# V's place as a fourth weight buffer for every other FFN group, in a fused adaLN, attention and SwiGLU kernel

## The chip, the cores and the metric

The kernel runs on one core of one Trainium2 chip. The metric is the device time in microseconds (us) of one execution, as a median of several runs. "TensorE" is PE in the profile, "VectorE" is DVE, "ScalarE" is ACT, and SPq is the queue on which the SyncE sequencer issues DMAs.

## The reference

Cut to what matters (S = 2048 rows, D = 1024, F = 3584, bf16):

```python
h = _layernorm(x) * (1 + ca) + sa
x = x + ga * attention(h, k_cache, v_cache, wq, wo)   # 32 heads, last 512 keys
h = _layernorm(x) * (1 + cb) + sb
x = x + gb * ((silu(h @ w_gate) * (h @ w_up)) @ w_down)
```

## The kernel before

The rows are done in four chunks of 512 (`cc` = 0 to 3). Attention for all chunks comes first; then the FFN, chunk by chunk. For each chunk the FFN runs over 7 groups (`fg`) of 512 columns of F. A group needs four weight tiles of 512 KB: two of `w_gate` (wg) and two of `w_up` (wu). They come from a pool of seven buffers:

```python
    pb_ = ctx.enter_context(tc.tile_pool(name="blkB", bufs=7))
    ...
    v_sb = const.tile([P, Hkv, WT, Dh + 32], BF16, name="v_sb")   # V, read by attention alone
    ...
    def load_gu(cc, fg):
        for nm, v in (("wg", wg_v), ("wu", wu_v)):
            for i in range(2):
                t = blkB(nm, [P, 4, 512])
                load(t, v[:, 4 * i:4 * i + 4, fg * 512:(fg + 1) * 512])
                gu_w[(cc, fg, nm, i)] = t

    def emit_gu(cc, f):                      # f = 4 * fg + fi, 28 of them a chunk
        ...
        ps = big("gu_ps")                    # two buffers in PSUM
        for n, nm in enumerate(("wg", "wu")):
            for dt in range(DT):             # 8 matmuls each
                nc.tensor.matmul(ps[:, n, :], lhsT=gu_w[(cc, fg, nm, dt // 4)][...],
                                 rhs=hT[("h2", cc)][:, dt, :], ...)
        nc.scalar.activation(out=g, in_=ps[:, 0, :], func=ACT.Silu)
        nc.vector.tensor_tensor(out=guT[(cc, fg)][:, fi, :], in0=ps[:, 1, :], in1=g, op=ALU.mult)
```

While the first FFN chunk runs, the second layer norm of the last chunk (`cc` = 3) is still being made. VectorE writes the normalized rows xn; four DMA transposes on SPq turn them into hT.

## Time and profile before

| what | before |
|---|---|
| time, median of the first 3 runs | 1285.66 us (1285.42 to 1287.39) |
| span of the profiled execution | 1282.7 us |
| PE busy | 99% |
| first gu_ps matmul / last d_ps matmul starts at | 673.97 / 1277.20 us |

The page's first part gives the engines' busy time and share of the span; its fourth part says what the last chain of waits consists of:

```profile
PE 1269.7 (99%) x7601; PEld 642.9 (50%) x7601; DVE 577.8 (45%) x1271; ACT 333.9 (26%) x433; POOL 1.2 (0%) x8
...
PE 95%; DMA 2%; DVE 1%; SPq 1%; ACT 0%; issue 0%; DVEq 0%
```

Matmuls overlap (each counts 0.379 us, at 0.216 us from start to start), so a busy share hides gaps. Starts are better to read. This is the timeline of PE (start, length, engine, line, operation, count, and in brackets the idle time before it and what ended it):

```profile
749.94 1.89 PE L1168 MATMUL gu_ps<-hT,wg 128*128 128x512 bf16 x8
751.66 1.03 PE L1168 MATMUL gu_ps<-hT,wu 128*128 128x512 bf16 x4
754.79 1.04 PE L1168 MATMUL gu_ps<-hT,wu 128*128 128x512 bf16 x4 [2.10 <-DMA wu<-in_B_w_up_dram]
755.66 1.89 PE L1168 MATMUL gu_ps<-hT,wg 128*128 128x512 bf16 x8
```

Eight matmuls take 1.72 us, 0.216 us each from start to start. The fourth wu matmul of f = 16 starts at 752.31, the fifth not at 752.53 but at 754.79. (The profile counts idle time from the modelled end of a matmul, 0.379 us after its start. So its 2.10 us of idle is a start-to-start distance of 2.48 us, and 2.26 us are lost.) The list of PE's waits after 640 us has this wait alone:

```profile
PE gu_ps L1168 <- DMA wu<-in_B_w_up_dram: 2.1, 1, 2.1
```

The timeline of SPq shows why the load came late:

```profile
732.00 0.37 SPq L664 DMA_DIRECT2D wu<-in_B_w_up_dram  x1
...
743.56 6.84 SPq L848 DMA_TRANSPOSE hT<-xn  x4
750.50 0.53 SPq L664 DMA_DIRECT2D wu<-in_B_w_up_dram  x1
```

The wu at 732.00 is the fourth tile of group 3, issued alone as soon as a buffer came free. That of group 4 could have gone at about 747.5, but it stands behind four transposes and goes at 750.50. Issuing these four takes the queue 6.84 us.

### The profile page before, as it was taken

What the parts mean: (1) busy time and instruction counts of PE and PEld (TensorE: products, weight loads), DVE (VectorE), ACT (ScalarE), POOL (GpSimd) and SP (SyncE); (2) the same over time, 40 slices, a digit from 0 to 9 for tenths busy, and PEclk for the clock granted to TensorE, in tenths of its full rate; (3) what the DMA queues carried; (4) which work ended last, traced back from release to release, by engine and by line L of the source; (5) the groups of instructions that cost most, each with busy time, mean ns of one, the idle gap of its engine ahead of it and who ended that gap; (6) DMA issues with size and microseconds to landing.
All of it is one profiled execution on the core that took longest, in us unless ns stands there. A gap on an engine that the chain in (4) does not pass through costs nothing.

```text
span 1282.7 us, 18139 instructions
## 1 busy us (share of the span) xinstructions
PE 1269.7 (99%) x7601; PEld 642.9 (50%) x7601; DVE 577.8 (45%) x1271; ACT 333.9 (26%) x433; POOL 1.2 (0%) x8
## 2 busy tenths in 40 slices
PE   8999999999999999999999999999999999999998
PEld 4555555555555555555554444444444444444444
DVE  4464467865577755576653642221212221221122
ACT  3543334333333433333341111011100111011100
POOL 0000000000000000000000000000000000000000
PEclk9999999999999999999999999999999999999999
DMA  9888476557355654445487484454536455454401
GB/s 293 269 204 232 152 154 167 141 149 195 91 129 155 144 148 140 123 142 131 132 207 221 142 234 150 140 189 147 181 102 216 143 165 164 135 193 134 146 21 48
DMA packets 280108, 204.21 MB, mean 159 GB/s; under 512 B 113865, under 2 KB 273609, under 8 KB 280018
## 3 DMA queue, kind: packets, MB, share of 16 engines
q1 hardware_dynamic: 275106, 198.78, 54.2%
q10 hardware_dynamic: 4912, 4.20, 1.0%
q8 instruction: 61, 1.00, 0.3%
q14 instruction: 29, 0.24, 0.1%
HBM read 174.08 MB, written 4.21 MB: 139 GB/s over the span
## 4 chain that ended last, share of the span: by engine, by line
PE 95%; DMA 2%; DVE 1%; SPq 1%; ACT 0%; issue 0%; DVEq 0%
PE gu_ps L1168 29%; PE a_ps L1096 17%; PE q_ps L1019 17%; PE d_ps L1188 15%; PE o_ps L1064 9%; PE s_ps L1032 8%; DMA wm<-in_w_mod_dram 1%; SPq L664 1%; DMA hT<-xn 0%; DMA modT<-row_d 0%; DMA wu<-in_B_w_up_dram 0%; PE row_ps L779 0%; PE q_ps L940 0%; DVE st L816 0%; SPq L848 0%; ACT pT L1034 0%
## 5 line engine op out<-in xcount | busy, mean ns | idle before, releaser
L1034 ACT ACTIVATE pT<-s_ps 128x1024 bf16<-128x1024 f32 x256 | 248.7, 1020 | 341.8 <-PE s_ps L1032 341.8
L1096 PE MATMUL a_ps<-wo,oT 128*128 128x512 bf16 x1024 | 241.9, 379 | 0.7 <-DVE acc L1102 0.7
L1019 PE MATMUL q_ps<-hT,wq 128*128 128x512 bf16 x1000 | 236.7, 379 | 0.3 <-DVE modT L755 0.3
L1168 PE MATMUL gu_ps<-hT,wu 128*128 128x512 bf16 x896 | 211.8, 379 | 2.1 <-DMA wu<-in_B_w_up_dram 2.1
L1168 PE MATMUL gu_ps<-hT,wg 128*128 128x512 bf16 x896 | 211.7, 379 | 0.0
L1174 DVE TENSOR_TENSOR guT<-gu_ps,sg 128x512 bf16<-128x512 f32 x112 | 77.4, 691 | 283.5 <-ACT sg L1173 283.5
L1173 ACT ACTIVATE sg<-gu_ps 128x512 bf16<-128x512 f32 x112 | 66.9, 597 | 490.9 <-PE gu_ps L1168 439.7
L1188 PE MATMUL d_ps<-wd,guT 128*128 128x512 bf16 (+2 forms) x952 | 194.2, 366 | 0.0
L916 DVE CAST qT<-q_ps 128x512 bf16<-128x512 f32 x128 | 88.3, 691 | 176.6 <-PE q_ps L1019 176.0
L1096 PEld LDWEIGHTS <-oT 128*128 128x128 bf16 x1024 | 99.9, 98 | 122.1 <-issue 1.9
L1019 PEld LDWEIGHTS <-wq 128*128 128x128 bf16 x1000 | 97.8, 98 | 117.8 <-issue 0.3
L1188 PEld LDWEIGHTS <-guT 128*128 128x128 bf16 x952 | 90.9, 98 | 102.9
L1064 PEld LDWEIGHTS <-pT 128*128 128x128 bf16 x2048 | 126.6, 98 | 30.6 <-issue 0.4
L1168 PEld LDWEIGHTS <-wu 128*128 128x128 bf16 x896 | 87.6, 98 | 108.1 <-DMA wu<-in_B_w_up_dram 2.6
L1168 PEld LDWEIGHTS <-wg 128*128 128x128 bf16 x896 | 87.7, 98 | 105.4
L1064 PE MATMUL o_ps<-v_sb,pT 128*128 128x130 bf16 x2048 | 137.1, 220 | 0.0
L1032 PE MATMUL s_ps<-qT,kT 128*128 128x512 bf16 x512 | 131.5, 379 | 0.6 <-ACT pT L1034 0.6
L1051 DVE TENSOR_TENSOR oq<-o_ps,rl 128x256 bf16<-128x256 f32 (+2 forms) x256 | 101.3, 420 | 4.3
L1192 DVE TENSOR_TENSOR f<-d_ps,gb_bc 128x512 f32<-128x512 f32 (+2 forms) x34 | 22.5, 661 | 147.0 <-PE d_ps L1188 147.0
L1104 DVE TENSOR_TENSOR acc<-a_ps,acc 128x512 f32<-128x512 f32 x64 | 44.1, 689 | 38.9 <-PE a_ps L1096 38.9
L1032 PEld LDWEIGHTS <-kT 128*128 128x128 bf16 x512 | 44.9, 98 | 31.7 <-issue 1.3
L816 DVE BATCH_NORM_STATS2 st<-x 128x6 f32<-128x512 bf16 x64 | 41.3, 680 | 2.9 <-DMA x<-in_A_x_dram 2.6
(75 smaller groups left out, 309.3 us busy)
## 6 DMA issues: line engine op xcount, KB each, us to landing
wq<-in_A_wq_dram SPq DMA_DIRECT2D x64, 512.0 KB, 4.1
wo<-in_A_wo_dram SPq DMA_DIRECT2D x64, 512.0 KB, 5.5
wg<-in_B_w_gate_dram SPq DMA_DIRECT2D x56, 512.0 KB, 5.1
wu<-in_B_w_up_dram SPq DMA_DIRECT2D x56, 512.0 KB, 3.8
wd<-in_B_w_down_dram SPq DMA_DIRECT2D x56, 512.0 KB, 6.4
wmr<-in_w_mod_dram SPq DMA_DIRECT2D x8, 1024.0 KB, 11.4
x<-in_A_x_dram SPq DMA_DIRECT2D x16, 256.0 KB, 5.7
wm<-in_w_mod_dram SPq DMA_DIRECT2D x4, 1024.0 KB, 10.5
```

What stands on the lines that cost most here:

```text
L916: nc.vector.tensor_copy(out=t, in_=q_ps)
L1019: nc.tensor.matmul(q_ps, lhsT=wq_tiles[(cc, h // 4, dt // 4)][:, dt % 4, (h % 4) * P:(h % 4 + 1) * P], rhs=hT[("h1", cc)][:, dt, :], start ...
L1032: nc.tensor.matmul(s_ps[:, i, :], lhsT=kT[:, kv, j * P:(j + 1) * P], rhs=qT[g], start=True, stop=True)
L1034: nc.scalar.activation(out=p[:, 2 * jj:2 * jj + 2, :], in_=s_ps, func=ACT.Exp, scale=scale)
L1051: nc.vector.tensor_tensor(out=dst, in0=ps[:, s0:s0 + cnt, 0:Dh], in1=sc, op=ALU.mult)
L1064: nc.tensor.matmul(o_slot["ps"][:, s_, :], lhsT=pT[g][:, j, t * P:(t + 1) * P], rhs=v_sb[:, kv, j, 0:VN], start=(j == 0), stop=(j == WT - 1))
L1096: nc.tensor.matmul(a_ps, lhsT=oT[(cc, 2 * q + i)][:, hh % 4, t * P:(t + 1) * P], rhs=wo_tiles[(cc, q, dh, i)][:, hh % 4, :], start=(hh == ...
L1104: nc.vector.tensor_tensor(out=acc[(cc, t)][:, dsl], in0=a_ps, in1=acc[(cc, t)][:, dsl], op=ALU.add)
L1168: nc.tensor.matmul(ps[:, n, :], lhsT=gu_w[(cc, fg, nm, dt // 4)][:, dt % 4, fi * P:(fi + 1) * P], rhs=hT[("h2", cc)][:, dt, :], start=(dt ...
L1173: nc.scalar.activation(out=g, in_=ps[:, 0, :], func=ACT.Silu)
L1174: nc.vector.tensor_tensor(out=guT[(cc, fg)][:, fi, :], in0=ps[:, 1, :], in1=g, op=ALU.mult)
L1188: nc.tensor.matmul(d_ps, lhsT=guT[(cc, f // 4)][:, f % 4, t * P:(t + 1) * P], rhs=wd_tiles[(cc, dh, f // 4)][:, f % 4, c0:c0 + w], start=( ...
```

## The change

V is not read after attention, so its place in the on-chip memory is free in the FFN. The intent is to give gate and up weights two full sets of four tiles: seven pool buffers, and V's place for the fourth tile of each odd group.

```diff
+    v_flat = v_sb.rearrange("p a b c -> p (a b c)")
+    v_blk = v_flat[:, 0:2048].rearrange("p (a b) -> p a b", a=4)
+
     def load_gu(cc, fg):
+
         for nm, v in (("wg", wg_v), ("wu", wu_v)):
             for i in range(2):
-                t = blkB(nm, [P, 4, 512])
+                spare = (cc * NFG + fg) % 2 == 1 and nm == "wu" and i == 1
+                t = v_blk if spare else blkB(nm, [P, 4, 512])
                 load(t, v[:, 4 * i:4 * i + 4, fg * 512:(fg + 1) * 512])
```

## The prediction

> **What bounds the kernel now.** TensorE. The page gives PE busy 1269.7 of 1282.7 us (99%), and the chain that ended last is 95% PE. Busy alone proves little; in the timeline eight 128x512 matmuls take 1.725 us, 215.6 ns each, at a granted clock of 1.00. [...] So in the FFN (from 674 us on) there is nothing to win but gaps between matmuls, and there is exactly one: at 752.3 us the next start comes 2.48 us later instead of 0.22 us. The list of PE's waits has it as the only one after 640 us: 2.1 us, "gu_ps <- DMA wu". PE's other idle time lies in the first 30 us, untouched.
>
> **Why that gap.** Seven buffers hold four tiles a group, so the fourth tile of a group can't be loaded until the first tile of the group before is read for the last time. The queue's timeline shows it: one wu alone is issued about 5.0 us before its need, lands in 3.8 us, and so arrives 1.15 us early, in group after group. Group 4 is the exception: its fourth buffer came free at 747.4 us, but in the queue's order it stands behind four transposes hT<-xn that are issued from 743.6 to 750.4 us as VectorE supplies xn. It was issued at 750.50, landed at 754.75 and was needed at 752.5.
>
> **What the change does.** No work is added: the same 112 gate and up loads of 512 KB, the same matmuls. In the built programs PE's order is the same; only the DMA queue's moves. All four tiles of a group now come in a row, two groups ahead, when the tiles of two groups before come free. By the order in the queue, group 4's four tiles are issued before the hT transposes (estimate: about 731 to 734 us, when group 2 ends, 18 us before use), group 5's just after them, at about 750.5, some 15 us before use.
> Risks: the first load into V's place waits for the last o_ps matmul (674.1 us) and stands ahead of four transposes oT<-oq, which were issued at 674.7 anyway and are needed about 20 us later. DMA share is 0.40 to 0.68 in these stages (windows).
>
> **How much is on the critical path.** Only the 2.1 to 2.3 us gap: it stands in the chain as DMA hT<-xn, then DMA wu, and from 754.79 us to the end the chain is PE without a pause. The other fourth tiles gain slack that nobody waits for.
>
> **Time.** 1285.66 - 2.3 = 1283.4 us, 0.2% faster. Range 1282.4 to 1285.2 (runs of before spread over 2 us). Faster by over 2%: 0.005; within 2%: 0.99; slower: 0.005.
>
> **What would show it.** PE's waits after 640 us: none (right), or the same or another DMA wait (wrong). Timeline at 750 us: gu_ps starts unbroken. wu loads issued over 10 us before use in every group. Clock and DMA bytes (204 MB) unchanged.
>
> **What would make it wrong.** A new wait elsewhere, from the moved order: oT transposes or wd loads late behind loads that wait for buffers, or hT transposes slowed by loads in flight, each seen as a PE wait for a DMA. Or matmuls that are slower when their weights lie where V was: mean start-to-start above 216 ns.

1285.66 us less the gap of 2.3 us is 1283.4 us. That nothing but gaps was to be won, because a matmul of this size could not start sooner after the last than these 215.6 ns, was the author's estimate.

## More of the kernel before

```python
    def ln_mod(key, dt, sc, sh):             # VectorE, needs the DMA transpose
        ln_affine(key, dt, hT[key][:, dt, :], sc, sh, False)

    def plan_late_ln(k, key, sc, sh):
        for t in range(QT):
            ...
            at(k + 10 + 2 * t, ln_rows, tt)          # xn
            at(k + 11 + 2 * t, ln_xpose, key, tt)    # DMA transpose hT<-xn on SPq
        at(k + 8, late_rstd)
        for dt in range(DT):
            at(k + 24 + dt, ln_mod, key, dt, sc, sh)
```

In the FFN the framework's scheduler is free to move these operations; it puts them much earlier than their step, beside f = 13 to 16 of the first chunk.

## The result, and the profile after

| | before | after |
|---|---|---|
| median, 6 runs each | 1286.62 us (1285.42 to 1288.03) | 1284.75 us (1283.85 to 1285.22) |
| ratio | | 0.9984, 95% interval 0.9971 to 0.9997 |
| span of the profiled execution | 1282.7 us | 1283.0 us |
| first s_ps matmul starts at | 26.46 us | 27.69 us |
| first gu_ps to last d_ps (starts) | 603.24 us | 601.96 us |

A ratio here is the mean time of one kernel's runs over that of the other's of the same rounds, so it is not quite the ratio of the medians.

The time lies in the predicted range. The two profiled executions differ the other way (1282.7 and 1283.0 us), because the first 30 us alone took 1.23 us longer in the second one, under a lower granted clock (0.94 before, 0.89 after, from the windows view), and a wait at about 91 us (see e11) another 0.26 us. So the FFN is compared by itself, from the first gu_ps to the last d_ps: 1.28 us shorter, where 2.26 us had been forecast.

PE's waits after 640 us, and PE's timeline, in the changed kernel:

```profile
PE gu_ps L1173 <- DVE guT L1179: 0.8, 1, 0.8
```

```profile
751.42 1.89 PE L1173 MATMUL gu_ps<-hT,wg 128*128 128x512 bf16 x8
753.15 1.89 PE L1173 MATMUL gu_ps<-hT,wu 128*128 128x512 bf16 x8
755.87 1.89 PE L1173 MATMUL gu_ps<-hT,wg 128*128 128x512 bf16 x8 [0.83 <-DVE guT L1179]
```

The load wait is gone: eight wu matmuls in a row at f = 16. But one step later, before f = 17, the start-to-start distance is 1.21 us, so 1.00 us are lost to a wait for VectorE. SPq did what was forecast. Group 4's two wu tiles go at 735.21, ahead of the transposes:

```profile
733.49 1.23 SPq L664 DMA_DIRECT2D wg<-in_B_w_gate_dram  x2
735.21 1.23 SPq L664 DMA_DIRECT2D wu<-in_B_w_up_dram  x2
736.94 3.96 SPq L664 DMA_DIRECT2D wd<-in_B_w_down_dram  x4
745.04 6.80 SPq L848 DMA_TRANSPOSE hT<-xn  x4
```

VectorE's timeline shows the new wait. First the kernel before, then the changed one:

```profile
749.06 0.69 DVE L1174 TENSOR_TENSOR guT<-gu_ps,sg 128x512 bf16<-128x512 f32 x1
752.46 1.38 DVE L856 TENSOR_SCALAR hT<-hT,modT 128x512 bf16<-128x512 bf16 x4 [2.71 <-DMA hT<-xn]
753.75 0.69 DVE L1174 TENSOR_TENSOR guT<-gu_ps,sg 128x512 bf16<-128x512 f32 x1
```

```profile
750.50 0.68 DVE L1179 TENSOR_TENSOR guT<-gu_ps,sg 128x512 bf16<-128x512 f32 x1
753.84 1.38 DVE L856 TENSOR_SCALAR hT<-hT,modT 128x512 bf16<-128x512 bf16 x4 [2.66 <-DMA hT<-xn]
755.14 0.68 DVE L1179 TENSOR_TENSOR guT<-gu_ps,sg 128x512 bf16<-128x512 f32 x1
```

Both kernels do the same: VectorE reaches the scale and shift of hT, waits there about 2.7 us for the DMA transposes, does four of them, and only then empties gu_ps of f = 15. The matmuls of f = 17 need that PSUM buffer, as there are two. In the kernel before, PE was waiting for the wu load at that very time, until 754.79, and guT was done at 754.44 (753.75 + 0.69), before PE came to f = 17. Without the load wait PE would have come there at 753.39 (751.66 plus 8 x 0.216): 1.05 us too early. So a second wait seemed to lie underneath the first. ScalarE had finished sg for this step at 750.74 in the kernel before and at 752.22 in the changed one (timeline of ACT), so it was VectorE, standing at hT until 752.46 and 753.84, that kept guT back.

### The profile page after: what moved, and what is told of

Read it like the earlier page. It is cut to its first block, busy times and chain, and to the rows that moved or that the text cites. A ratio compares the mean times of both kernels' runs of the same rounds, so it can differ in the third digit from the quotient of the medians.

```text
span 1283.0 us, 18137 instructions
## 1 busy us (share of the span) xinstructions
PE 1270.0 (99%) x7601; PEld 643.1 (50%) x7601; DVE 577.3 (45%) x1271; ACT 333.9 (26%) x433; POOL 1.2 (0%) x8
## 2 busy tenths in 40 slices
DMA packets 280108, 204.21 MB, mean 159 GB/s; under 512 B 113865, under 2 KB 273609, under 8 KB 280018
## 4 chain that ended last, share of the span: by engine, by line
PE 96%; DMA 2%; DVE 1%; SPq 0%; ACT 0%; issue 0%; DVEq 0%
PE gu_ps L1173 29%; PE a_ps L1096 17%; PE q_ps L1019 17%; PE d_ps L1193 15%; PE o_ps L1064 9%; PE s_ps L1032 8%; DMA wm<-in_w_mod_dram 1%; DMA hT<-xn 1%; PE q_ps L940 0%; DMA modT<-row_d 0%; PE row_ps L779 0%; SPq L664 0%; PE mod_ps L753 0%; DVE st L816 0%; ACT pT L1034 0%; PE h_ps L927 0%
## 5 line engine op out<-in xcount | busy, mean ns | idle before, releaser
L1173 PE MATMUL gu_ps<-hT,wu 128*128 128x512 bf16 x672 | 163.3, 379 | 0.0
L1173 PEld LDWEIGHTS <-wu 128*128 128x128 bf16 x672 | 65.8, 98 | 79.3
L1173 PE MATMUL gu_ps<-hT,v_sb 128*128 128x512 bf16 x224 | 57.5, 379 | 0.0
```

## The experiments

Theory A: the change removes the load wait of group 4, and only that load mattered; a wait of 1.0 us for VectorE, which had lain under it, comes to light. Its rivals: the new wait is made by the moved loads; the load was late for another reason; the eighth buffer helps everywhere a little. "FFN" in the table is the start of the first gu_ps to that of the last d_ps. "Lost" is the start-to-start distance less 0.216 us. Every run gave the correct result.

| run | time, median | before beside it | ratio (95%) | FFN | lost in the FFN, to |
|---|---|---|---|---|---|
| before (first trace) | | | | 603.24 | 2.26, DMA wu |
| after (first trace) | | | | 601.96 | 1.00, DVE guT |
| e1_before_mod | 1285.71 | 1287.35 | 0.9987 (0.9974 to 1.0001) | 604.79 | 2.13, DMA wu |
| e2_after_again | 1284.41 | 1287.35 | 0.9975 (0.9962 to 0.9989) | 601.71 | 0.75, DVE guT |
| e3_after_mod | 1283.24 | 1287.35 | 0.9966 (0.9953 to 0.9980) | 600.96 | 0 |
| e4_spare_g1_g3 | 1284.20 | 1287.35 | 0.9973 (0.9960 to 0.9987) | 601.71 | 0.75, DVE guT |
| e5_before_again | 1286.12 | 1285.52 | 1.0006 (0.9992 to 1.0019) | 603.00 | 2.03, DMA wu |
| e6_before_fill | 1285.70 | 1285.52 | 1.0001 (0.9987 to 1.0015) | 603.12 | filled |
| e7_before_b6 | 1302.18 | 1285.52 | 1.0156 (1.0114 to 1.0199) | 619.57 | 20 waits, DMA wu |
| e8_after_b6 | 1287.07 | 1285.52 | 1.0009 (0.9993 to 1.0024) | 605.23 | 2.58, DMA wu |
| e9_spare_g1 (one run) | 1286.36 | 1286.06 | | 604.98 | 2.31, DMA wu |
| e10_before_late | 1283.22 | 1286.06 | 0.9977 (0.9962 to 0.9993) | 600.96 | 0 |
| e11_after_mod_cb1 | 1282.22 | 1286.06 | 0.9970 (0.9956 to 0.9983) | 601.04 | 0.08, at f = 16 |

e1 to e4 ran on one chip, e5 to e8 on another, e9 to e11 on a third. e9 was profiled once and not timed further; its state is unknown.

### e1 and e3: the VectorE operations later, in the kernel before and in the changed one

The eight hT operations of the last chunk and the guT operations are held to the order in which the program names them. That puts the former into the FFN of the second chunk.

```diff
     def ln_mod(key, dt, sc, sh):
+        if key == ("h2", NTC - 1):
+            tc.keep_in_program_order(nc.vector.tensor_scalar(out=hT[key][:, dt, :], ...same...))
+            return
         ln_affine(key, dt, hT[key][:, dt, :], sc, sh, False)
 ...
-        nc.vector.tensor_tensor(out=guT[(cc, fg)][:, fi, :], in0=ps[:, 1, :], in1=g, op=ALU.mult)
+        tc.keep_in_program_order(nc.vector.tensor_tensor(...same...))
```

Expected of e1:

> Seven buffers as before, but the eight VectorE operations that finish hT (scale and shift after the DMA transposes) stand later in VectorE's order, so that no guT stands behind them at about 754 us. Theory A (a second wait, of VectorE behind the transposes, lay hidden under the load wait): the load wait stays, start-to-start gap 2.48 us at the second half of wu of group 4, nothing else; first gu_ps to last d_ps stays 603.2 us; time as before within 0.1%. Rival B (the second wait was made by the moved loads and has nothing to do with this order): the same here. Rival C (the late wu load was late because VectorE stalled, not because of the buffer and the queue): the gap shrinks below 1 us.

Measured: the load wait stayed, 2.13 us lost, with nothing else behind it. So VectorE's stall at hT had not made it, and rival C falls. (The edit leaves the xn operations in place, but once the first transpose had gone, the queue of the kernel before waited for them for 0.33 us alone.) The FFN was not 603.2 but 604.79 us. That surprise is in the next part.

Expected of e3:

> The changed kernel with the eight VectorE operations later, as in e1. Theory A: no gap over 0.235 us after 640 us, first gu_ps to last d_ps 600.7 us, that is the whole 2.48 - 0.22 = 2.26 us of before plus nothing; 1.0 us faster than the changed kernel. Rival B (the moved loads slow the transposes or PE in some other way): a wait of about 1 us is left at this place, under another name.

Measured: no wait of PE after 640 us is left, and the FFN takes 600.96 us. That is 603.24 less 2.26; the 600.7 in the expectation was a slip of the sum. VectorE's timeline in e3 shows guT waiting for nothing but ScalarE where it had stood behind hT:

```profile
750.02 0.69 DVE L1184 TENSOR_TENSOR guT<-gu_ps,sg 128x512 bf16<-128x512 f32 x1
751.65 0.69 DVE L1184 TENSOR_TENSOR guT<-gu_ps,sg 128x512 bf16<-128x512 f32 x1 [0.95 <-ACT sg L1183]
755.11 0.69 DVE L1184 TENSOR_TENSOR guT<-gu_ps,sg 128x512 bf16<-128x512 f32 x1 [2.76 <-ACT sg L1183]
```

The four kernels make a square: either cure alone leaves a wait (2.13 us with the VectorE order alone, 0.75 to 1.00 us with the buffer alone), both leave none. The moved loads are not to blame, as they are the same in e3.

### e2 and e4: the change once more, and V's place in two groups alone

> The changed kernel once more, beside the others on one chip. Both theories: one gap of 1.2 us (start to start) before the first matmul of f = 17, put down to DVE guT; first gu_ps to last d_ps 602.0 us, 1.26 us under before; time 0.1 to 0.2% under before, with the rest of the difference from the first 30 us.

Measured: one gap again, 0.97 us from start to start, so 0.75 us lost instead of 1.00; the FFN is 601.71 us. The size of this wait depends on when the transposes land: counted from the first gu_ps, the last one landed at 78.27 us in the first trace and at 78.01 us here, 0.26 us earlier, and the wait is 0.25 us shorter. The time came out 0.25% under before, more than the FFN explains; see below.

```diff
-                spare = (cc * NFG + fg) % 2 == 1 and nm == "wu" and i == 1
+                spare = cc * NFG + fg in (1, 3) and nm == "wu" and i == 1
```

> V's place is used by groups 1 and 3 alone, the other 12 odd groups have the seven buffers as before. Theory A (only group 4's load counted): as the changed kernel, one gap of 1.2 us at f = 17, first gu_ps to last d_ps 602.0 us, although the fourth tiles of groups 6 and later land with 1.15 us to spare again. Rival D (the eighth buffer helps a little in every group, for instance by relieving the DMA queue): longer than 602.2 us.

Measured: the same gap and the same FFN as e2, to 0.01 us, and a median 0.2 us apart. Twelve of the fourteen uses of V's place gain nothing that can be seen here.

### e9: V's place in group 1 alone

The same edit with `in (1,)`. SPq's order from group 2 on is then as before, and group 4's last tile stands behind the transposes again.

> V's place is used by group 1 alone; from group 2 on the DMA queue's order is as in before, so group 4's fourth tile is again issued behind the four hT transposes. Theory A: the load wait is back, start-to-start gap 2.2 to 2.5 us at wu of f = 16, first gu_ps to last d_ps 603.0 to 603.3 us (or 1.7 us more where the clock drops). Rival G (it is enough that the first groups are loaded earlier): a gap of 1.0 to 1.2 us put down to DVE guT, 601.7 to 602.0 us, as in e4.

The queue in e9's timeline, as it was in the kernel before:

```profile
743.69 6.90 SPq L848 DMA_TRANSPOSE hT<-xn  x4
750.69 0.53 SPq L664 DMA_DIRECT2D wu<-in_B_w_up_dram  x1
```

Measured in one look: the load wait is back, with 2.31 us lost, and the matmuls after it were slow again, as in e1 (eight took 2.90 us instead of 1.89; FFN 604.98 us). So it is the place of group 4's load in the queue that counts.

### e10: another order of the transposes, with no eighth buffer

The kernel before with e1's edit, and the four late xn operations held to program order too, which moves the transposes on SPq behind group 4's load. (The diff is cut to its new part.)

```diff
-            at(k + 10 + 2 * t, ln_rows, tt)
+            at(k + 10 + 2 * t, ln_rows, tt, True)   # True: xn kept in program order
```

> Seven buffers, no use of V's place, but the four xn operations and with them the hT transposes of the last chunk, and the hT scale and shift, keep their program order and so come later, after group 4's fourth tile. Theory A (the order in the DMA queue, not the number of buffers, made the wait): the 2.48 us gap at f = 16 is gone without the eighth buffer. The transposes now stand among other fourth tiles with 1.15 us to spare, so a smaller wait at another group is possible; I expect at most 1 us in all, first gu_ps to last d_ps 601.0 to 602.0 us. Rival H (seven buffers make group 4 late by themselves): the 2.48 us gap stays.

The queue in e10's timeline (cut):

```profile
747.50 0.37 SPq L664 DMA_DIRECT2D wu<-in_B_w_up_dram  x1
...
776.07 1.25 SPq L856 DMA_TRANSPOSE hT<-xn  x1
```

Measured: group 4's load went at 747.50, no wait after 640 us, FFN 600.96 us as in e3, and 1283.22 us (e3, on another chip: 1283.24). I had feared a smaller wait at another group; none came. Seven buffers are enough when the four transposes do not stand in a row ahead of a load that has about 1.15 us to spare. The eighth buffer makes the kernel indifferent to that order, which is another way to the same gain, but it cannot cure the VectorE wait.

### e7 and e8: one buffer fewer

```diff
-    pb_ = ctx.enter_context(tc.tile_pool(name="blkB", bufs=7))
+    pb_ = ctx.enter_context(tc.tile_pool(name="blkB", bufs=6))
```

> The kernel before with 6 buffers in place of 7, so two tiles a group, not one, come just in time. Theory A (7 buffers were enough everywhere else because the fourth tile lands 1.15 us early): now wu0 has about 4.1 us from issue to need and wu1 5.0 us, and a pair issued together lands in about 4.5 and 5.2 us, so PE waits about 1 us in each of some 21 groups without attention work beside them: first gu_ps to last d_ps about 620 to 625 us, time about 1.5% over before. Rival D (buffers hardly matter to this kernel): within 0.3% of before.

> The changed kernel with 6 buffers in place of 7: with V's place it has 7 in odd groups, so one tile a group comes just in time, as in before. Theory A: about as before with 7 (load wait of 2 us at group 4, first gu_ps to last d_ps 603 to 605 us), so here the same change is worth about 1.5% against e7. Rival D: equal to e7.

PE's waits after 640 us, e7 first, then e8 (what waited for what, us in total, times, longest):

```profile
PE gu_ps L1168 <- DMA wu<-in_B_w_up_dram: 13.0, 20, 2.9
```

```profile
PE gu_ps L1173 <- DMA wu<-in_B_w_up_dram: 2.4, 1, 2.4
```

Measured: with six buffers PE waits in 20 of the 28 groups, and the kernel is 1.56% slower by the ratio, which takes the mean and so one long run, or 1.3% by the medians. (The waits were shorter than the 1 us that I had expected for most groups, and the FFN at 619.57 us was just under the range that I gave. One of e7's four runs took 1314.39 us at a mean clock of 0.993; the median is 1302.18.) The same change as the studied one takes nearly all of it back: 1.0009 of the kernel with seven. (Its FFN, 605.23 us, is just above the expected 603 to 605; the half-clock stretch told below is in it.) So a buffer is worth 1.2 to 1.5% at six and 0.2% at seven. At seven the fourth tile lands 1.06 to 1.30 us early within a chunk, wherever a landing is recorded and no attention work stands between, except behind the transposes.

### e5 and e6: what a gap costs besides its length

In e1 the matmuls right after the load wait ran at half speed: the first four took 1.67 us, 0.42 us each from start to start instead of 0.216, under a granted clock of 0.51. Windows of e1 (stretch, length, busy time and count of PE, PEld, DVE, ACT and POOL, granted clock, DMA share, GB/s), then its timeline:

```profile
753.00:755.60 2.60, 0.63 (x4) 0.10 (x2) 0.00 (x0) 0.00 (x0) 0.00 (x0) 1.00 0.93 300
755.60:759.00 3.40, 3.40 (x9) 1.16 (x10) 0.69 (x1) 0.60 (x1) 0.00 (x0) 0.51 1.10 354
759.00:769.00 10.00, 9.95 (x47) 4.57 (x47) 1.38 (x2) 1.48 (x3) 0.00 (x0) 1.00 0.20 50
```

```profile
755.60 1.88 PE L1173 MATMUL gu_ps<-hT,wu 128*128 128x512 bf16 x4 [1.97 <-DMA wu<-in_B_w_up_dram]
757.27 2.77 PE L1173 MATMUL gu_ps<-hT,wg 128*128 128x512 bf16 x8
```

Eight matmuls took 2.77 us instead of 1.89. In the first trace of before, the granted clock was 1.00 in the same place. I took up theory E: an idle stretch of about 2 us sometimes costs a stretch of half clock (in e1, after 1.97 us, it did; in before, after 2.10 us, it did not). Why it does so at one time and not at another is not shown by any trace; a guess at it is cut from the expectation of e5. The kernel before was run again, unchanged (e5), and with ten matmuls of constants in the gap (e6; the eight wu matmuls of this step are held to program order too):

```diff
+                if here and dt == 4:             # cut; "here" is f = 16 of the first chunk, n = 1
+                    for _ in range(10):
+                        tc.keep_in_program_order(nc.tensor.matmul(
+                            fill_ps, lhsT=ones_bf, rhs=warm_w, start=True, stop=True))
```

> The kernel before, byte for byte, to have a second trace of it and its run-to-run spread on one chip. In the trace of e1, which keeps the load wait, the matmuls after the wait ran at half clock for 3.4 us and cost 1.7 us more; in the first trace of before they did not. Theory E (an idle stretch of 2.1 us sometimes costs a stretch of half clock[...]): times spread over 3 to 4 us, 1285.5 to 1289.5; in the trace first gu_ps to last d_ps is either 603.2 us or about 604.9 us, nothing between. Rival F (e1's slow stretch came from its edit): 603.2 us and full clock at 755 us, times as the first three runs, 1285.4 to 1287.4.

> The kernel before with ten matmuls of constants put between the first four and the last four wu matmuls of f = 16, where PE waits: 10 x 0.216 = 2.16 us of work in a gap of 2.26 us, so PE is hardly idle but the load is as late as before. The wait's own length is not won back. Theory E: first gu_ps to last d_ps 603.2 us, full clock throughout the FFN, and the times lose their slow runs: spread about 2 us like the changed kernel's, median about 1 us under before's. Rival F: times and spread as before's.

Measured: e5's trace is of the kind without the drop, 603.00 us, and its five times spread over 3.0 us, as theory E had it; those of before beside it, nine runs of the same kernel, spread over 2.2 us. e6 took 603.12 us in the FFN, so without the 1.7 us of a drop, but its time and spread (1285.05 to 1287.14) were those of before beside it (1284.60 to 1286.79). The expected gain of 1 us was not there, so e6 does not show that the drop costs before much on this chip.

What the traces show together is this. In e1 and e8 the granted clock fell to half right after a load wait, to 0.51 from 755.60 to 759.00 us and to 0.50 from 756 to 759 us, and in e9 the matmuls were as slow there (eight took 2.90 us instead of 1.89). The gaps ahead of it were 2.13, 2.58 and 2.31 us. The price was about 1.7 us: the FFN of e1, e8 and e9 is 1.69 to 1.71 us longer than e3's plus the gap. In before, with a gap of 2.26 us, the granted clock stayed at 1.00 (windows, 752 to 769 us), and the FFN of before and e5 (2.03 us) is e3's plus the gap to within 0.02 us. Nor is there such a price where the gap was 1.0 us or less: the FFN of after, e2, e4, e10 and e11 is e3's plus the gap to within 0.01 us; e6, with its gap filled, took 603.12 us. So the length of the gap alone does not tell when the clock falls (2.13 us fell, 2.26 did not), and what decides it was not shown. No trace of the unchanged kernel caught the fall; there are two.

### e11: one more wait of the same kind removed

Every trace up to e10 has one more gap before the FFN. At about 91 us PE waits for acc, which stands on VectorE behind an operation that adds 1 to the second norm's scale, and that operation waits for a DMA. In the kernel before, PE first, then VectorE:

```profile
91.93 1.89 PE L1096 MATMUL a_ps<-wo,oT 128*128 128x512 bf16 x8 [0.73 <-DVE acc L1102]
90.52 0.17 DVE L802 TENSOR_SCALAR modT<-modT 128x8 f32<-128x8 f32 x1 [3.36 <-DMA modT<-row_d]
90.60 0.69 DVE L816 BATCH_NORM_STATS2 st<-x 128x6 f32<-128x512 bf16 x1
91.20 0.67 DVE L1102 COPY acc<-a_ps 128x512 f32<-128x512 f32 x1
```

It is the same pattern, so e11 is e3 with this addition 12 steps later and held to program order:

```diff
         if add_one:
-            nc.vector.tensor_scalar(out=dst, in0=dst, scalar1=1.0, scalar2=None, op0=ALU.add)
+            at(16 * n + 28, plus_one, dst)       # cut; plus_one is the same operation, as a step of its own
```

> e3 with one more operation moved: the VectorE operation that adds 1 to the scale for the second norm, which waits at about 87 to 91 us for a DMA and holds up acc and so PE (gap of 1.0 to 1.8 us at 91 us in every trace so far), stands 12 steps later. Theory A (in-order VectorE behind an operation that waits for a DMA makes PE wait): this gap falls to 0.3 us or less, first gu_ps to last d_ps stays 601.0 us, first s_ps to first gu_ps 646.6 us against 647.5 to 648.2; time about 1 us under e3, so 0.3% under before. Rival: the gap stays, because it is a load or PSUM that PE waits for.

Measured: the gap is gone, first s_ps to first gu_ps is 646.61 us, and the median is 1282.22 us, 0.9970 of the kernel before and the lowest of all that were run. It was timed beside the kernel before alone, not beside the changed kernel or e3, so the 1.0 us between its median and e3's is not a measured ratio; the gap itself (1.0 to 1.4 us lost in the traces on e3's chip, nothing in e11's) is. That e3 is faster than the changed kernel is measured on one chip: e3's slowest run, 1283.60 us, is under e2's fastest, 1283.65.

## Why the prediction was right or wrong

- **TensorE bounds the kernel, and the FFN has one gap to win.** Right. Eight matmuls take 1.72 us, 0.216 us each from start to start, before and after, and in e3 no wait of PE is left after 640 us. That they could not go faster than 0.216 us was not shown.
- **The gap comes from the fourth tile's place behind the transposes in the queue.** Right. e9 brings the wait back by restoring that order, and e4 and e10 remove it, the latter without any buffer.
- **"The other fourth tiles gain slack that nobody waits for."** Right. e4 leaves twelve of fourteen uses out and loses nothing.
- **"PE's other idle time lies in the first 30 us, untouched."** Not quite: 0.9 us were lost at 91 us, which is the wait that e11 removes. The change did not touch it.
- **The added risks** did not come true. The first load into V's place was issued at 675.52, the transposes oT<-oq from 676.21, and no PE wait followed. The transposes hT<-xn took the queue 6.80 us, and 6.84 before. Nor are matmuls slower with weights from V's place: four of them take 0.86 us there (750.56 to 751.42 in the changed kernel's timeline), 0.216 us each.
- **"Only the 2.1 to 2.3 us gap ... from 754.79 us to the end the chain is PE without a pause."** This step failed, by its size. A chain of waits names what came last at each step. It does not show what was late underneath. The FFN gained 1.28 us and not 2.26, because VectorE, standing at hT until the transposes landed, held the PSUM buffer of f = 15 until 1.05 us after PE would have wanted it. The lines were there to be read in the trace of before: hT at 752.46, then guT at 753.75. e3 shows that with VectorE's order mended too, the whole 2.26 us come.
- **"PE's waits after 640 us: none (right), or the same or another DMA wait (wrong)."** Neither: the wait that came was for VectorE. The two other signs came: every wu load is issued 14.8 us or more before its use, and the DMA bytes are 204.21 MB in both.
- **"1285.66 - 2.3 = 1283.4 us, 0.2% faster. Range 1282.4 to 1285.2"** The measured 1284.75 lies within. It is 1.35 us above the point, of which 1.00 us is the VectorE wait. The rest is less than what runs of one kernel differ by. Before itself had a median of 1286.62 over six runs, 1.0 us above the 1285.66 of its first three. So luck has a part in the good number: of the 1.9 us between the medians the FFN gives 1.28, and 1286.62 - 1.28 = 1285.3 would have been just outside the range.
- **What stays open** is the part of the measured differences that the FFN does not give: 0.6 us in the first comparison of medians, and 1.4 us in e2's (2.9 us, of which its FFN gives 1.53). The mean granted clock that is recorded with every run, to three decimals, points to the clock. On the chip of e1 to e4 it was 0.9966 in the nine runs of before, 0.9974 in e2 and 0.9976 in e3 (means). Span times clock, as a rough estimate of the time at full clock, is 1281.1 us for before, 1280.8 for e1, 1279.3 for e2 and 1278.3 for e3. That is 0.4, 1.8 and 2.8 us under before, where the FFN without a drop of the clock gives 0.1, 1.5 and 2.3. Where in a run the clock was lower is not recorded. It can be the half-clock stretch after the long gap, which cost 1.7 us where it fell (e1, e8, e9) and was not seen in the two traces of the changed kernel (FFN 601.96 and 601.71 us); how often it falls in the kernel before was not measured, and e6 did not show it. Or it can be the first 30 us, which vary by 1.75 us between traces (first s_ps at 25.99 to 27.74 us).

## What to carry to other kernels

When one wait is taken out of a chain, look in the old trace at what each other engine was doing at that moment: compute when the waiting engine would have arrived without the wait, and check that every buffer that it needs was free by then. Here, on VectorE and on SPq, an operation that was not ready or took long held up what stood behind it: guT behind 2.7 us of waiting for a transpose, which cost PE 0.75 to 1.00 us, and a load behind four transposes, issued at 750.50 us and not at about 747.5, which cost 2.26 us (2.03 to 2.31 in e1, e5 and e9). So place an operation that waits for a DMA late, well after its data can have landed; here mending the order alone (e10) gained as much in the FFN as buffer and order together (e3), and more than the buffer alone. Adding a buffer paid here where tiles arrived late in most turns (1.3 to 1.6% from six to seven); where they were already early by about 1.15 us it paid only for the one turn that something else delayed.
